# Groups 0 to 4 plain with all attention units among them, and two pairs of groups at the end, in a fused attention and token/channel mixer on one core

## The chip, the core and the metric

The kernel runs on one core of a Trainium2 chip. A core has TensorE (PE: matmuls, with weight loads shown apart as PEld), VectorE (DVE), ScalarE (ACT), GpSimd (POOL) and SyncE (SP), which here issues most DMAs. Engines run their instructions in order, each its own queue, and wait for each other through semaphores. SBUF is the on-chip memory, PSUM the eight accumulator banks that PE writes. The metric is the device time in microseconds of one execution; lower is better.

## The reference

Eight batches, eight heads, 576 rows, 64 columns a head. The attention is linear: softmax of q over the head's columns, softmax of k over the rows, then two small products. A mixer over tokens and a mixer over channels follow; all in fp32.

```python
q_s = softmax(q, axis=-1); k_s = softmax(k, axis=2)
kv = einsum('bhsd,bhse->bhde', k_s, v)
x = einsum('bhsd,bhde->bhse', q_s, kv)          # then (8, 576, 512)
h = np.maximum(x.transpose(0, 2, 1) @ w_tok1, 0.0) @ w_tok2      # 576 -> 256 -> 576
u = x + h.transpose(0, 2, 1)
h2 = np.maximum(u @ w_ch1, 0.0) @ w_ch2                          # 512 -> 1536 -> 512
out = u + h2
```

## The kernel before

The work has two halves. The first makes u in 32 *units*: a unit is one batch b and one slice j of 128 of the 512 channels (two heads). Its stages are the softmax of k and q (`softmax_k`, `softmax_q`: DVE, ACT, POOL), the transposed q (`stage_qT`, through DRAM for the later units), kv (`stage_kv`), y (`stage_y`), h1 (`stage_h1`) and two halves of u (`stage_u`). `begin` loads a unit two units ahead.

The second half is the channel mixer. The 8 x 576 rows of u are cut into nine *groups* of 512 rows, which do not fall together with the batches. For a group, ch1 gives 12 rows of 128 hidden channels (f = 0 to 11), ch2 adds them to the four output tiles of 128 channels. Each fp32 operand is kept as a high and a low part (`split`: ACT copies the high one, DVE subtracts it), and a product takes three matmuls (high x high, low x high, high x low). A plain ch1 of one f is 4 x 3 = 12 matmuls of 512 columns, a plain ch2 of one f as many. The main loop goes over `steps` (group, f): it issues ch1 of this step, then whatever `todo` holds for it (unit stages, put there by `put` with a step number), then ch2 of the step before. ch1's relu, high part on ACT and low part on DVE (lines 490 and 491), stands between the two.

Two by two blocks of a product can be had with seven products in place of eight (Strassen and Winograd's scheme), with sums of weight blocks and of data blocks. Weight blocks and their sums are made once and written to DRAM (`keep_blocks`, `keep_sums` for ch1, `keep_out`, `keep_out_sums` for ch2), and each product loads its weights, 256 KB, into a ring of buffers (`load_product`, `weights_used`). Before, this is used in two ways:

- Groups 0, 1 and 2 are plain in ch1 and ch2.
- Groups 3 to 6 (`G_S` = 3) use it in ch1 alone, and take the two blocks of data from the two halves of the same group: `pair_a` and `pair_b` do two f at a time by seven products of 6 matmuls on 256 columns, with five sums on DVE; ch2 is plain.
- Groups 7 and 8 use it in both, with the blocks from the two groups: `both_groups` does six pairs of f by seven products of 6 matmuls on 512 columns (part a), and then for each of seven products all six pairs (part b). Data sums are made ahead by `row_sum`, `data_sums`, `wide_sums` and `wide_split`; in part b `operand` makes each operand up to `AHEAD` products before its use.

The units run among the steps: batch 2 at two steps a unit, batches 3 to 7 at three steps a unit (line 1015), so up to the last of groups 2 to 6. The order within each engine comes from the framework's scheduler, which takes the program's order and its own estimate of durations; so an instruction can move past others, and the order is fixed before the kernel runs.

Of the kernel before, what the change touches and what calls it, by code (L numbers as in the profile page):

```python
# [20 lines left out]
def attn_mixer_kernel(ctx: ExitStack, tc: tile.TileContext, q, k, kt, v, wt, out, dims):  # L21
# [16 lines left out]
    G_S = 3  # L38
# [3 lines left out]
    KEEP = (5.5, 7.5, 37, 38.5, 40, 41.5)  # L42
    AHEAD = 12
# [11 lines left out]
    ps_o = ctx.enter_context(tc.tile_pool(name="ps_o", bufs=NJ, space=bass.MemoryType.PSUM))  # L55
    ps_h = ctx.enter_context(tc.tile_pool(name="ps_h", bufs=4, space=bass.MemoryType.PSUM))
# [54 lines left out]
    main_pools = ctx.enter_context(ExitStack())  # L111

    def c2_rows(f0, f1):
        late = main_pools.enter_context(tc.tile_pool(name=f"late{f0}", bufs=1))
# [9 lines left out]
    c2_rows(0, F_HEAD)  # L124
    part = const.tile([P, NJ, CW], F32, name="part")
# [42 lines left out]
    def load_unit(b, j):  # L168
        n = b * NJ + j
        u = {"b": b, "j": j, "n": n, "early": n < NE}  # L170
# [104 lines left out]
    whole = {}  # L275

    def load_pair(f):
# [6 lines left out]
        split(*(w[:, i : i + 2].rearrange("p f m -> p (f m)") for w in (wh, wl)), load_wide(AT_C2 + f), nc.vector)  # L284

    def load_ch(f):
# [6 lines left out]
        split(*c2_row(f), load_weights(AT_C2 + f), nc.vector)  # L293
# [149 lines left out]
    uT = [slots[i] for i in (0, 1, 2, 1, 0, 2, 1, 0, 2)]  # L443
    assert len(uT) == NG
# [3 lines left out]
    def stage_u(u, half):  # L448
# [16 lines left out]
        for g, a0, a1 in ((b, n0, min(n1, edge)), (b + 1, max(n0, edge), n1)):  # L465
            if a0 < a1:
                at = b * S + a0 - g * CW
                uh, ul = (x[:, j, at : at + a1 - a0] for x in uT[g])
# [57 lines left out]

    def keep_out(p):

        scratch_v[p] = dpool.tile([P, 7, 2, 2 * P], F32, name=f"v{p}")
# [5 lines left out]
    def keep_out_sums(p):  # L535

        hi = stg.tile([P, CW, 2], U32, name="stg").rearrange("p n w -> p (n w)").bitcast(F32R)
        lo = stg.tile([P, CW, 2], U32, name="stg").rearrange("p n w -> p (n w)").bitcast(F32R)
        a = f32(hi).rearrange("p (f m) -> p f m", f=2)
        (wh, wl), i = c2[2 * p]  # L540
        nc.gpsimd.tensor_tensor(a, f32(wh[:, i : i + 2]), f32(wl[:, i : i + 2]), op=ALU.add)
        s = f32(lo).rearrange("p (k m) -> p k m", k=4)
        (a11, a21), (a12, a22) = ([a[:, f, x * 2 * P : (x + 1) * 2 * P] for x in range(2)] for f in range(2))
# [5 lines left out]
        for x, w in enumerate((hi, lo)):  # L549
            nc.sync.dma_start(scratch_v[p][:, P5 : P3 + 1, x, :], f32(w).rearrange("p (k m) -> p k m", k=4))  # L550


    ring, T, tf, odd, h_slots = [], [], [], [], []

    def stage_pair_pools(f0):
        if f0 == F_MORE:
            c1_pools[F_LAST].close()
        c1_pools[f0].close()
        if f0 == 0:
            pool = ctx.enter_context(tc.tile_pool(name="pairs_a", bufs=1, side="right", reuse_waits="tile"))  # L560
# [12 lines left out]
    FIRST = (P1, P5, P2, P3, P6, P7, P4)
    GA, GB = NG - 2, NG - 1
    turn_of = [FIRST] + [TURN] * (NP - 1)
    loads = [(scratch_w, p, e) for g in range(G_S, GA) for p in range(NP) for e in TURN]
    n_main = len(loads)
    loads += [(scratch_w, p, e) for p in range(NP) for e in turn_of[p]]
    loads += [(scratch_v, p, e) for e in TURN for p in range(NP)]
    slot_of = [i % 8 if i < n_main else (i - n_main) % 6 for i in range(len(loads))]  # L580
    after, to_load, last_in = {}, [], {}
    for i, x in enumerate(slot_of):
        (after.setdefault(last_in[x], []) if x in last_in else to_load).append(i)
        last_in[x] = i

    def load_at_place(i):
        where, p, e = loads[i]
        nc.sync.dma_start(f32(ring[slot_of[i]].rearrange("p n m -> p (n m)")), where[p][:, e].rearrange("p x m -> p (x m)"))

    def load_product():  # L590
        load_at_place(to_load.pop(0))

    at_product, at_h = [0], [0]

    def next_weights():
        w = ring[slot_of[at_product[0]]]
        at_product[0] += 1
        return w

    def weights_used():  # L600
        for i in after.get(at_product[0] - 1, ()):
            load_at_place(i)

    rows = {}

    def rows_of(g):
        if g not in rows:
            if g % 2:
                rows[g] = [part[:, n : n + 2, :] for n in (0, 2)]
            else:  # L610
                rows[g] = [
                    stg.tile([P, CW, 2], U32, name="stg").rearrange("p n w -> p (n w)").bitcast(F32).rearrange("p (n w) -> p n w", n=2)
                    for _ in range(2)
                ]
        return rows[g]

    def row_sum(g, n, eng):
        uh, ul = (x[:, n, :] for x in uT[g])
        eng.tensor_tensor(rows_of(g)[n // 2][:, n % 2, :], f32(uh), f32(ul), op=ALU.add)

    A, Bq = slice(0, HW), slice(HW, CW)

    def data_sums(g, which):
        lo_rows, hi_rows = rows_of(g)
        b11, b12, b21, b22 = lo_rows[:, :, A], lo_rows[:, :, Bq], hi_rows[:, :, A], hi_rows[:, :, Bq]
        f0, f1 = (halves(x) for x in tf)
        sub = ALU.subtract
        for i in which:
            o, a, b = ((f0, b12, b11), (f1, b22, f0), (f0, b22, b12), (f0, b21, f1))[i]
            nc.vector.tensor_tensor(o, a, b, op=sub)  # L630
            split(T[0][:, i], T[1][:, i], tf[i == 1], nc.vector)

    def product(g, e, t, cols):
        w = next_weights()
        uh, ul = uT[g]
# [527 lines left out]
```

## Time and profile before

| | |
|---|---|
| three runs | 794.04, 794.77, 797.56 us (median 794.77) |
| the profiled execution | 796.62 us, of which the span from the first to the last instruction is 794.8 us |
| granted TensorE clock | 0.998 of full |
| bytes moved by DMA | 174.83 MB, 220 GB/s over the span |

In the profile, a group of instructions is shown by line, engine, operation and its tiles (out<-in); a tile's buffer numbers are left out. Matmuls overlap in the pipeline, so the duration of one is longer than the pace of a row of them; the pace is read from start to start, or from a chain of a known count. Idle time of an engine is given with what released it.

The page's slices of the span (40, each 19.9 us), in tenths of busy time:

```profile
PE   3899999999999999999999999999999999999998
...
DVE  7979998978788874878688657888987557667971
```

### The profile page before, as it was taken

What the parts mean: (1) busy time and instruction counts of PE and PEld (TensorE: products, weight loads), DVE (VectorE), ACT (ScalarE), POOL (GpSimd) and SP (SyncE); (2) the same over time, 40 slices, a digit from 0 to 9 for tenths busy, and PEclk for the clock granted to TensorE, in tenths of its full rate; (3) what the DMA queues carried; (4) which work ended last, traced back from release to release, by engine and by line L of the source; (5) the groups of instructions that cost most, each with busy time, mean ns of one, the idle gap of its engine ahead of it and who ended that gap; (6) DMA issues with size and microseconds to landing.
All of it is one profiled execution on the core that took longest, in us unless ns stands there. A gap on an engine that the chain in (4) does not pass through costs nothing.

```text
span 794.8 us, 13455 instructions
## 1 busy us (share of the span) xinstructions
PE 769.0 (97%) x4824; PEld 670.9 (84%) x4824; DVE 618.1 (78%) x1101; ACT 341.9 (43%) x744; POOL 180.7 (23%) x130
## 2 busy tenths in 40 slices
PE   3899999999999999999999999999999999999998
PEld 2688888877888888899999999989999998888886
DVE  7979998978788874878688657888987557667971
ACT  4666433444454443434353334434444324346610
POOL 0000000011111352122211111232422320536640
PEclk9999999999999999999999999999999999999999
DMA  9655644158879785587879777999978543667776
GB/s 304 187 174 166 224 150 171 44 171 278 273 243 336 232 286 177 144 282 210 238 213 287 226 219 216 288 339 314 316 233 270 161 134 115 195 189 198 192 207 196
DMA packets 151459, 174.83 MB, mean 220 GB/s; under 512 B 51297, under 2 KB 98017, under 8 KB 151393
## 3 DMA queue, kind: packets, MB, share of 16 engines
q1 hardware_dynamic: 145056, 161.65, 67.2%
q10 hardware_dynamic: 6336, 12.32, 4.1%
q8 instruction: 38, 0.62, 0.3%
q14 instruction: 29, 0.23, 0.1%
HBM read 131.47 MB, written 42.47 MB: 219 GB/s over the span
## 4 chain that ended last, share of the span: by engine, by line
PE 70%; DVE 11%; issue 7%; DMA 7%; ACT 2%; POOL 1%; SPq 1%; DVEq 0%; POOLq 0%; ACTq 0%
PE ps_o L694 20%; PE ps_h L645 14%; PE ps_h L768 7%; PE ps_o L768 7%; PE ps_h L464 6%; PE ps_h L422 4%; PE ps_h L487 4%; PE ps_h L357 2%; DMA q_t<-in_q 2%; DMA stg<-whole 1%; PE ps_h L430 1%; PE ps_o L464 1%; PE ps_o L882 1%; DMA w<-stg 1%; DVE q_t L340 1%
## 5 line engine op out<-in xcount | busy, mean ns | idle before, releaser
L694 PE MATMUL ps_o<-h,c2h 128*128 128x512 f32 x544 | 184.2, 398 | 2.9 <-ACT h L490 1.9
L694 PEld LDWEIGHTS ps_o<-h,c2h 128*128 128x128 f32 x544 | 101.4, 188 | 23.8 <-ACT h L490 3.0
L694 PE MATMUL ps_o<-h,c2l 128*128 128x512 f32 x272 | 106.0, 393 | 0.0
L318 POOL TENSOR_TENSOR k_t<-k_t,dg 128x640 f32<-128x640 f32 x24 | 41.6, 1735 | 217.6 <-ACT dg L317 182.1
L135 POOL TENSOR_TENSOR ql<-q_t,qh 128x640 fp32r<-128x640 f32 x24 | 38.4, 1599 | 182.3 <-PE ps_o L694 104.2
L645 PE MATMUL ps_h<-th,ring 128*128 128x256 f32 x384 | 72.3, 283 | 0.0
L645 PEld LDWEIGHTS ps_h<-th,ring 128*128 128x128 f32 x384 | 60.1, 191 | 0.0
L694 PEld LDWEIGHTS ps_o<-h,c2l 128*128 128x128 f32 x272 | 51.3, 188 | 8.6
L487 PE MATMUL ps_h<-uh,c1l 128*128 128x512 f32 x144 | 56.2, 390 | 0.0
L487 PE MATMUL ps_h<-ul,c1h 128*128 128x512 f32 x144 | 56.2, 390 | 0.0
L487 PE MATMUL ps_h<-uh,c1h 128*128 128x512 f32 x144 | 56.1, 392 | 0.0
L645 PE MATMUL ps_h<-uh,ring 128*128 128x256 f32 x288 | 54.4, 282 | 0.6 <-DVE c L672 0.6
L645 PE MATMUL ps_h<-tl,ring 128*128 128x256 f32 x192 | 54.3, 283 | 0.0
L645 PEld LDWEIGHTS ps_h<-uh,ring 128*128 128x128 f32 x288 | 46.5, 190 | 2.8 <-DVE c L672 0.8
L471 ACT CAST uh<-ps_h 128x320 fp32r<-128x320 f32 (+4 forms) x76 | 24.4, 334 | 52.1 <-PE ps_h L464 32.1
L336 ACT ACTIVATE q_t<-q_t 128x640 f32<-128x640 f32 x32 | 23.6, 738 | 46.1 <-DVE q_t L327 43.1
L326 DVE TENSOR_REDUCE st<-q_t 128x10 f32<-128x640 f32 x32 | 26.1, 815 | 22.2 <-DMA q_t<-in_q 22.2
L490 ACT ACTIVATE h<-ps_h 128x512 fp32r<-128x512 f32 x36 | 21.5, 598 | 49.5 <-PE ps_h L487 42.0
L645 PE MATMUL ps_h<-ul,ring 128*128 128x256 f32 x144 | 40.6, 282 | 0.0
L645 PEld LDWEIGHTS ps_h<-tl,ring 128*128 128x128 f32 x192 | 36.8, 192 | 0.0
L472 DVE TENSOR_TENSOR ul<-ps_h,uh 128x320 fp32r<-128x320 f32 (+4 forms) x76 | 27.4, 370 | 9.0 <-ACT uh L471 8.8
L135 DVE TENSOR_TENSOR qtl<-q_t,qth 128x512 fp32r<-128x512 f32 (+1 forms) x48 | 25.6, 566 | 8.1 <-ACT qth L134 7.3
(319 smaller groups left out, 2070.2 us busy)
## 6 DMA issues: line engine op xcount, KB each, us to landing
ring<-w SPq DMA_DIRECT2D x210, 256.0 KB, 3.7
ring<-v SPq DMA_DIRECT2D x42, 256.0 KB, 3.0
kt_t<-in_kt SPq DMA_DIRECT2D x32, 320.0 KB, 3.7
q_t<-in_q SPq DMA_DIRECT2D x32, 320.0 KB, 3.7
v_t<-in_v SPq DMA_DIRECT2D x32, 320.0 KB, 4.5
stg_w<-in_w SPq DMA_DIRECT2D x18, 512.0 KB, 6.0
k_t<-in_k SPq DMA_DIRECT2D x24, 320.0 KB, 4.9
q<-cv_s SPq DMA_DIRECT2D x24, 320.0 KB, 3.2
```

The costliest lines, as they stand in the source:

```text
L135: lo_eng.tensor_tensor(lo, src, f32(hi), op=ALU.subtract)
L318: nc.gpsimd.tensor_tensor(kx, kx, dg.unsqueeze(1).broadcast_to([P, C1, P]), op=ALU.subtract)
L326: nc.vector.tensor_reduce(st[:, 0, :], qt, axis=AX.X, op=ALU.max)
L336: nc.scalar.activation(qc, qc, AF.Exp)
L422: nc.tensor.matmul(y[:, 0:TOK], a, w, start=(i == 0), stop=(i == len(mm) - 1))
L464: nc.tensor.matmul(t[:, 0:N], a, w, start=(i == 0), stop=(i == len(mm) - 1))
L471: nc.scalar.copy(uh, src).ins,
L472: nc.vector.tensor_tensor(ul, src, f32(uh), op=ALU.subtract).ins,
L487: nc.tensor.matmul(t, a[:, n, :], w, start=(i == 0), stop=(i == 3 * NJ - 1))
L645: nc.tensor.matmul(t[:, cols], a, b[:, n], start=(i == 0), stop=(i == 5))
L694: m = nc.tensor.matmul(o, a[:, cs], w, start=(first and i == 0), stop=(last and i == 2))
L768: nc.tensor.matmul(o, a, b, start=first and i == 0 and (n == 0 or not one), stop=last and i == 2 and (n == 1 or not one))
```

## The change

The uses of the seven products are changed. `G_S` becomes 5: groups 0 to 4 are plain in ch1 and ch2, and the last four groups are two pairs, (5, 6) and (7, 8), both by `both_groups`, which is called for round 0 and round 1. `pair_a`, `pair_b` and their pools are gone. What moves with it:

- Units: batches 3 to 6 run at two steps a unit, all within the steps of groups 2 to 4 (36 steps); batch 7's four units run among the items of round 0, a unit every 12 items (`SPACE`). An item is one product of 6 matmuls; a round has 84.
- u of groups 5 to 8 is not split in `stage_u` but copied by ACT (`stay`) and written to DRAM (`u_kept`); `make_first`, `make_second` and `make_third` load it, make the data sums and split them. For round 0 that is in the last steps of group 4; for round 1 in the last part of round 0. The residual is loaded again (`residuals`).
- In a round, the products that share an accumulator add up in PSUM (P1, P6, P7, P4 in one bank, P5 and P3 in another, P2 in a third), with copies of the partial sums in between; before, each product had a bank of its own and DVE summed them. Six banks serve the products, two the units (`bank_pools`).
- Operands of part b take the places of u and of a part of c2; the differences for P6 and P4 are made by POOL when they are needed; `AHEAD` is 9 for 12. Parts a and b interleave by a fixed list (`items`).
- c2's pieces are also written to DRAM when they are loaded (`whole_out`), and `keep_out_sums` reads them back; POOL's sum for it is gone. The steps at which blocks and sums are kept change (`BLOCKS1`, `SUMS1`, `BLOCKS2`, `SUMS_AT`).

```diff
-    G_S = 3
+    G_S = 5
+    NR = (NG - G_S) // 2
-    KEEP = (5.5, 7.5, 37, 38.5, 40, 41.5)
-    AHEAD = 12
+    AHEAD = 9
+    SUMS_AT = (6.5, 11.5, 16.5, 21.5, 26.5, 29.5)
+    BLOCKS1, SUMS1, BLOCKS2 = (18, 20, 22, 24, 26, 28), (20.5, 24.5, 28.5, 32.5, 37.5, 42.5), (6, 11, 16, 21, 26, 29)
+    RES_AT = 31
+    SPACE = ((7, 8, 1, 12), (8, 8, 0, 0))
...
     def load_ch(f):
...
-        split(*c2_row(f), load_weights(AT_C2 + f), nc.vector)
+        t = load_weights(AT_C2 + f)
+        split(*c2_row(f), t, nc.vector)
+        if f % 2 == 0:
+            whole_out[f // 2] = dpool.tile([P, 2 * CW], F32, name=f"out{f}")
+        nc.scalar.dma_start(whole_out[f // 2][:, f % 2 * CW : (f % 2 + 1) * CW], t.bitcast(F32))
...
+                if g >= len(uT):
+                    if g not in u["kept"]:
+                        u["kept"][g] = [at, at, stay()]
+                    k0, k1, x = u["kept"][g]
+                    nc.scalar.copy(x[:, k1 - k0 : k1 - k0 + a1 - a0], t[:, a0 - n0 : a1 - n0])
...
+    TURN = (P1, P5, P6, P2, P7, P3, P4)
+    items = [("a", 0, e) for e in TURN[:5]]
+    for p in range(1, NP):
+        items += [("a", p, P1), ("a", p, P5), ("a", p - 1, P4), ("a", p - 1, P3), ("a", p, P6), ("a", p, P2), ("a", p, P7)]
+    tail = [("b", c, e) for e in TURN for c in range(NP)]
+    items += tail[:2] + [("a", NP - 1, P4), ("a", NP - 1, P3)] + tail[2:]
...
+    def make_first(r):
+
+        g = G_S + 2 * r
+        ready[r] = []
+        for k in range(2):
+            b11, b12, b21, b22 = (h_of[2 + i][:, 1] if k and r else row_place() if i or r else sum_place() for i in range(4))
+            for t, (i, n) in ((b11, (0, k)), (b12, (1, k)), (b22, (1, 2 + k)), (b21, (0, 2 + k))):
+                nc.sync.dma_start(t, u_kept[g + i][n])
+            t0 = sum_place()
+            t1 = sum_place() if r else b11
+            split(*of_first[k], b11, nc.vector)
+            vec(t0, b12, b11, op=sub)
+            split(*of_T[0][k], t0, nc.vector)
+            vec(t1, b22, t0, op=sub)
+            split(*of_T[1][k], t1, nc.vector)
+            split(*of_second[k], b21, nc.vector)
+            vec(b12, b22, b12, op=sub)
+            vec(b21, b21, t1, op=sub)
+            ready[r].append((b12, b21, b22))
...
+        def operand():
...
+            if e in (P6, P4):
+                t = sum_place()
+                pl(t, h[:, 3], h[:, 0], op=sub)
+                if e == P4:
+                    pl(t, h[:, 2], t, op=sub)
...
+            if not end and kind == "b" and done_b[0] == N_MOST:
+                make_first(r + 1)
+            if not end and kind == "b" and done_b[0] == N_MOST + 8:
+                make_second(r + 1)
...
-    steps += [(g, f) for g in range(2, GA) for f in range(NF)]
+    steps += [(g, f) for g in range(2, G_S) for f in range(NF)]
...
+        elif b < 7:
+            at = [n0 + -1 + 2.0 * (n - 3 * NJ) + x for x in (0, 0.5, 1, 1.5, 2)]
         else:
-            at = [n0 - 1 + (b - 3) * NF + 3 * j + x for x in (0, 0.5, 1, 1.5, 2)]
+            break
...
-    both_groups()
+    hidden_pools()
+    bank_pools()
+    make_second(0, (3,))
+    for r in range(NR):
+        both_groups(r, laters[r])
```

Three places show how the order on an engine moves. The first is PE at the start of group 3. Before, it runs the products of `pair_a` (`uh`, `ul`: the parts of u; `th`, `tl`: the parts of the data sums; `ring`: the loaded weights):

```order
L645 MATMUL ps_h<-uh_125,ring_3103 128x256 x2
L645 MATMUL ps_h<-ul_126,ring_3103 128x256
L645 MATMUL ps_h<-uh_125,ring_3103 128x256 x2
L645 MATMUL ps_h<-ul_126,ring_3103 128x256
L645 MATMUL ps_h<-th,ring_3104 128x256 x2
L645 MATMUL ps_h<-tl,ring_3104 128x256
```

At the same place in the changed kernel, group 3's first ch1 follows y of a unit (L437) and runs on 512 columns with the weights in SBUF (`c1h`, `c1l`):

```order
L437 MATMUL ps_h<-w1tl,qh 128x256
L517 MATMUL ps_h<-uh_125,c1h_115 128x512
L517 MATMUL ps_h<-uh_125,c1l_116 128x512
L517 MATMUL ps_h<-ul_126,c1h_115 128x512
L517 MATMUL ps_h<-uh_125,c1h_115 128x512
L517 MATMUL ps_h<-uh_125,c1l_116 128x512
```

The matmuls of 256 columns with loaded weights have become matmuls of 512 columns that load nothing from DRAM.

The second place is SP at the start of round 0 in the changed kernel. `u_129` to `u_132` are the rows kept in DRAM of groups 5 to 8, L812 is a residual, L637 a ring load, L195, L186 and L412 belong to units:

```order
L812 DMA part<-u_130 128x512
L812 DMA stg<-u_129 128x512
L812 DMA rows_5266<-u_130 128x512
L812 DMA rows_5265<-u_130 128x512
L195 DMA v_t<-in_v 128x10x64
L186 DMA k_t<-in_k 128x640
L412 DMA q_5920<-cv_s 128x4x160
L812 DMA part<-u_129 128x512
L812 DMA stg<-u_129 128x512
L637 DMA ring_5257<-w_1973 128x512
L812 DMA part<-u_129 128x512
L637 DMA ring_5258<-w_2145 128x512
```

The scheduler has moved the residual loads, which the program issues at item 31, to the start of the round, ahead of the first ring loads that follow the eight made before the round; `part` and `stg` are also the buffers from which group 4's output is written.

The third place is DVE in the last part of round 0, where the operands for round 1 are made (`c2l`, `ul`: low parts of operands; L823: output sums; L675, L678: data sums of `make_first`; `hb`: the hidden rows or rows of u in their place):

```order
L143 TENSOR_TENSOR c2l_121<-hb_5450,c2h_120 128x512
L143 TENSOR_TENSOR ul_126<-stg,uh_125 128x512
L823 TENSOR_TENSOR part<-b_5461,part 128x512
L823 TENSOR_TENSOR part<-b_5460,part 128x512
L143 TENSOR_TENSOR ul_126<-hb_5449,uh_125 128x512
L143 TENSOR_TENSOR ul_128<-sum_5270,uh_127 128x512
L143 TENSOR_TENSOR ul_128<-sum_5272,uh_127 128x512
L143 TENSOR_TENSOR ul_128<-sum_5269,uh_127 128x512
L143 TENSOR_TENSOR ul_126<-part,uh_125 128x512
L823 TENSOR_TENSOR part<-b_5462,part 128x512
L675 TENSOR_TENSOR sum_5271<-part,sum_5270 128x512
L678 TENSOR_TENSOR stg<-part,stg 128x512
```

From the second of these rows to the last split for round 1 stand 28 rows, six of them output sums (L823); in the kernel before no second pair follows, and the rows have no counterpart.

More of the change, by code (lines that the diff above doesn't have):

```diff
@@ L600, in weights_used @@
[L600 to L631, printed above, removed]
@@ new lines, in attn_mixer_kernel, with pair_pools @@
+    ring, spare_rows, sums, h_of = [], [], [], []
+    def pair_pools():
+        c1_pools[0].close()
+        pool = ctx.enter_context(tc.tile_pool(name="pairs_a", bufs=1, side="right", reuse_waits="tile"))
+        ring.extend(pool.tile([P, 4, P], F32R, name=f"ring{i}") for i in range(8))
+        spare_rows.extend(part[:, n, :] for n in range(NJ))
+        spare_rows.extend(pool.tile([P, CW], F32, name=f"rows{i}") for i in range(2))
+        stays[:] = (pool.tile([P, CW], F32, name=f"stay{i}") for i in range(2))
+        sums.extend(pool.tile([P, CW], F32, name=f"sum{i}") for i in range(4))
@@ L756, in attn_mixer_kernel @@
-    b21_of = {}
-    def wide_split(i, k):
-        src = (first_diff[k:], wide_sum[k:], beside[k:], [b21_of.get(k)])[i][0]
-        split(*wide_T(i, k), src, nc.vector)
-    def six(w, pieces_h, pieces_l, outs, first, last):
-        for n in range(2):
-            o = outs[n % len(outs)]
-            one = len(outs) == 1
-            for i, (a, b) in enumerate(((w[:, n], pieces_h[n]), (w[:, 2 + n], pieces_h[n]), (w[:, n], pieces_l[n]))):
-                nc.tensor.matmul(o, a, b, start=first and i == 0 and (n == 0 or not one), stop=last and i == 2 and (n == 1 or not one))
@@ new lines, in bank_pools, with relu, six @@
+    def bank_pools():
+        banks.close()
+        pool = ctx.enter_context(tc.tile_pool(name="bk", bufs=1, space=bass.MemoryType.PSUM))
+        t = {i: pool.tile([P, CW], F32, name=f"b{i}") for i in (2, 3, 5, 4, 0, 1)}
+        places.extend(t[i] for i in range(6))
+        pu = ctx.enter_context(tc.tile_pool(name="pu", bufs=2, space=bass.MemoryType.PSUM))
+        unit_banks[0] = ((pu, "pu"),)
+    def relu(c):
+        nc.scalar.activation(c, c, AF.Relu)
+    def six(w, pieces_h, pieces_l, outs, first, last, which=(0, 1)):
+        one = len(outs) == 1
+        for n in which:
+            for i, (a, b) in enumerate(((w[:, n], pieces_h[n]), (w[:, 2 + n], pieces_h[n]), (w[:, n], pieces_l[n]))):
+                nc.tensor.matmul(
+                    outs[0 if one else n], a, b,
+                    start=first and i == 0 and (n == 0 or not one),
+                    stop=last and i == 2 and (n == 1 or not one),
+                    skip_group_check=True,
+                )
@@ L794, in operand, with both_groups @@
+    at_product = [0]
+    def both_groups(r, later):
+        ga = G_S + 2 * r
+        end = r == NR - 1
+        sets = [places[0:2], places[2:4]]
+        made, done_b, hidden = [0], [0], [0]
+        order = [(c, e) for _, c, e in tail]
         def operand():
             i = made[0]
[L796 removed]
+            if i == len(order):
                 return
[L798 removed]
+            c, e = order[i]
             made[0] += 1
[L800 removed]
@@ L908, in attn_mixer_kernel @@
+        if not end:
+            make_third(r + 1)
+        assert not later, later
     units = {}
```

520 lines of the change are left out of this document (219 added, 301 removed).

## The prediction

> **What bounds the kernel now.** I read the page's busy rows first, then the stretches of the span, then what TensorE (PE) waited for.
>
> ```profile
> span 794.8 us, 13455 instructions
> PE 769.0 (97%) x4824; PEld 670.9 (84%) x4824; DVE 618.1 (78%) x1101; ACT 341.9 (43%) x744; POOL 180.7 (23%) x130
> ```
>
> PE is busy for all but 25.8 us. The next view cuts the span by stage; its columns are the stretch, its length, and the busy time (and instructions) of PE, PE's weight loads, VectorE (DVE), ScalarE (ACT) and GpSimd (POOL), then the granted clock, the DMA share and GB/s.
>
> ```profile
> 0.00:78.00 78.00, 60.18 (x445) 50.74 (x446) 66.44 (x151) 48.66 (x113) 1.94 (x17) 0.98 0.68 212
> 78.00:155.00 77.00, 77.00 (x353) 64.22 (x353) 72.88 (x109) 32.98 (x53) 3.62 (x2) 1.00 0.42 148
> 155.00:240.00 85.00, 81.99 (x501) 68.49 (x500) 70.19 (x130) 38.93 (x88) 13.47 (x8) 1.00 0.76 233
> 240.00:331.70 91.70, 91.49 (x539) 77.51 (x539) 68.90 (x122) 39.25 (x86) 29.34 (x18) 1.00 0.75 236
> 331.70:669.00 337.30, 336.10 (x2451) 308.93 (x2451) 258.26 (x481) 135.77 (x328) 80.00 (x49) 1.00 0.79 242
> 669.00:735.00 66.00, 66.00 (x296) 54.79 (x296) 44.81 (x64) 30.74 (x52) 31.17 (x24) 1.00 0.65 182
> 735.00:794.80 59.80, 56.25 (x249) 46.24 (x247) 36.59 (x49) 15.55 (x28) 21.15 (x13) 1.00 0.69 199
> ```
>
> The idle time lies in the first 78 us (17.8), in 155 to 240 (3.0) and at the end (3.5). The clock is full. In 331.7 to 669 (groups 3 to 6) PE loses 1.2 us, in 669 to 735 nothing. So the kernel is bound by the number and pace of its matmuls, and the change is worth what it does to those, less every gap that it opens. All gaps behind 155 us but the tail are these, in order of time (idle time and releaser in brackets):
>
> ```profile
> 165.02 0.50 PE L694 MATMUL ps_o<-h,c2h 128*128 128x512 f32 x1 [0.96 <-ACT h L490]
> ...
> 173.69 0.50 PE L694 MATMUL ps_o<-h,c2h 128*128 128x512 f32 x1 [0.76 <-ACT h L490]
> ...
> 193.87 1.20 PE L694 MATMUL ps_o<-h,c2h 128*128 128x512 f32 x4 [1.00 <-DVE h L491]
> ```
> ```profile
> 529.28 0.50 PE L645 MATMUL ps_h<-uh,ring 128*128 128x256 f32 x2 [0.62 <-DVE c L672]
> ...
> 534.41 0.50 PE L464 MATMUL ps_h<-w2h,hl 128*128 128x256 f32 x2 [0.59 <-DVE hl L438]
> ```
>
> (0.5 us of tiny ones apart.) In a plain group PE waits for the relu of the hidden rows, when ACT or DVE come to it late.
>
> **The change, part by part.**
>
> 1. *The width of the products.* Before, groups 3 to 6 do ch1 by seven products on 256 columns: 4 groups x 6 pairs of rows x 7 x 6 = 1008 matmuls.
>
> ```profile
> L645 PE MATMUL ps_h<-th,ring 128*128 128x256 f32 x384 | 72.3, 283 | 0.0
> L645 PE MATMUL ps_h<-uh,ring 128*128 128x256 f32 x288 | 54.4, 282 | 0.6 <-DVE c L672 0.6
> L645 PE MATMUL ps_h<-tl,ring 128*128 128x256 f32 x192 | 54.3, 283 | 0.0
> L645 PE MATMUL ps_h<-ul,ring 128*128 128x256 f32 x144 | 40.6, 282 | 0.0
> ```
>
> 384+288+192+144 = 1008. Their durations overlap, so I take the pace from the chain that ended last, where 24 in a row stand with their sum:
>
> ```profile
> 331.91 2.87 PE ps_h L645 x24
> ...
> 698.77 5.44 PE ps_h L768 x24
> ```
>
> A matmul of 256 columns takes 119.6 ns, one of 512 takes 226.7. In columns nothing is saved: before, 3 plain groups x 288 + 4 x (126 + 144) + 504 = 2448 matmuls of full width; after, 5 x 288 + 2 x 504 = 2448. The seventh product is won on one more ch2 pair and given back by two plain ch1. What is left is width: 1008 x 0.1196 = 120.6 us become 504 x 0.2267 = 114.3: **-6.3 us**. (The Trainium skill speaks against this: "TensorE: Matmul & The Clock Gate", section "Back-to-back issue gap", gives an isolated matmul N/2.4 ns and about 2.5 ns more. By it 504 pairs save 504 x 2.5 ns = 1.3 us, and the sum below would be 5.0 us later. The trace's paces differ from it, 119.6 and 226.7 ns against its 109.2 and 215.8.)
>
> 2. *ch2 between narrow products.* Starts of ch2 between such products:
>
> ```profile
> 642.36 0.40 PE L694 MATMUL ps_o<-h3h,c2l 128*128 128x512 f32 x1
> ...
> 644.66 0.39 PE L694 MATMUL ps_o<-h3l,c2h 128*128 128x512 f32 x1
> ```
>
> Ten steps in 2.30 us are 230 ns each. The 288 matmuls of ch2 of groups 5 and 6 become products at 226.7: **-1.0** (bounds 0 and -2.0, if groups 3 and 4 gain it too).
>
> 3. *Gaps that go.* The two at 529 and 534 lie in work that is gone: **-1.2**. What could be late in their place is part 5.
>
> 4. *Loading.* load_pair and load_ch now also write each c2 piece to DRAM, so cv buffers are held longer.
>
> ```profile
> whole<-cv_s ACTq DMA_DIRECT2D x4, 256.0 KB, 3.7
> ```
>
> That is c1's copy now, and this is what DVE waited for it, 0.5 us in all:
>
> ```profile
> L395 DVE STREAM_TRANSPOSE cv_s<-q_t 128x640 f32<-128x640 f32 x24 | 20.1, 837 | 0.7 <-DMA whole<-cv_s 0.5
> ```
>
> DVE is busy 72.88 of 77 us in 78 to 155, so what is late there stays late. Four more such copies: the far end is 4 x (3.7 - 0.7) = 12 us, if DVE had nothing beside the split (0.7) to do meanwhile; but it works on the other buffer. I take the nearest row: **+0.5** (0 to 12; below nothing only by another order, of which I see no sign).
>
> 5. *Plain groups with all units among them.* Groups 2 to 4 are 36 steps, 864 x 0.2267 = 195.9 us. A unit's own PE time follows from groups 3 to 6: 337.3 - 120.6 - 576 x 0.230 = 84 us for 16 units, 5.3 each. So 16 units in plain groups make a stretch of 281 us with one unit in two steps, where it was three. Before ran two-step spacing in batch 2 alone:
>
> ```profile
> 158.00:198.00 40.00, 37.21 (x217) 30.31 (x216) 33.60 (x60) 16.92 (x39) 6.28 (x4) 1.00 0.72 224
> 198.00:238.00 40.00, 39.78 (x248) 34.29 (x247) 32.11 (x63) 19.86 (x45) 7.19 (x4) 1.00 0.84 258
> ```
>
> It lost 2.79 and 0.22 us of 40. Two of the first window's gaps (165, 173.7) lie where load_ch still runs; I take the second: 281 / 40 x 0.22 = **+1.5**, with ends 0 and 281 / 40 x 2.79 = 19.6. The far end is a rival below.
>
> 6. *Into round 0.* SP issues eight residual rows, some into buffers that wait for the output of group 4, ahead of the second set of ring loads.
>
> ```profile
> ring<-w SPq DMA_DIRECT2D x210, 256.0 KB, 3.7
> ...
> out<-part ACTq DMA_DIRECT2D x14, 256.0 KB, 4.5
> ```
>
> The cover is eight loaded products, 8 x 6 x 0.2267 = 10.9 us, and two units' PE time. Four sums of 0.69 (row in 8), 4.5 to land and 3.7 to load are 11.0 after the last ch2: **0**, up to +3.
>
> 7. *Units among products.* Products now add up in one PSUM bank, so a product waits for ACT's copy of the one before it; the order leaves two to three products, 2.7 to 4.1 us, between. The longest operation of a unit on DVE and a copy from PSUM on ACT:
>
> ```profile
> L340 DVE TENSOR_TENSOR q_t<-q_t,st 128x640 f32<-128x640 f32 x32 | 30.1, 942 | 0.4
> ```
> ```profile
> L836 ACT COPY hb<-ps_o 128x512 f32<-128x512 f32 x4 | 2.3, 582 | 0.0
> ```
>
> 0.58 and 0.94 fit into 2.7; three long operations ahead of a copy do not (3.4). Nothing to two gaps like that at 193.87 (1.00) in each of four units are 0 to +8; I take one gap in all, as two-step spacing gave one in 178 to 240: **+1.0**.
>
> 8. *The turn to round 1.* While P7, P3 and P4 of round 0 end, DVE must make the operands of round 1.
>
> ```profile
> L135 DVE TENSOR_TENSOR ul<-hb,uh 128x512 fp32r<-128x512 f32 x10 | 9.4, 967 | 1.8 <-ACT uh L134 1.8
> ...
> L904 DVE TENSOR_TENSOR stg<-ps_o,stg 128x512 f32<-128x512 f32 x2 | 1.4, 692 | 6.8 <-PE ps_o L768 6.8
> ...
> L135 DVE TENSOR_TENSOR x2l<-hb,x2h 128x512 fp32r<-128x512 f32 x1 | 0.7, 681 | 0.0
> ```
> ```profile
> L135 DVE TENSOR_TENSOR tl<-tb,th 128x512 fp32r<-128x512 f32 x4 | 4.7, 1207 | 0.0
> ```
>
> From the split of the first new row (its place is read by product 23 of the 42) DVE has 28 rows: six output sums and 22 operations between SBUF tiles. At 0.69 they take 19.3 us, at 0.967 25.4, at 1.207 30.7. PE has 19 products, 25.8 us. So 0 to 30.7 - 25.8 = +4.9; by the middle row it just fits: **+1.0**.
>
> Round 1 is like the old last pair (66.00 of 66.00 busy) with fewer sums on DVE, and the tail is the same. DVE loses the five sums of pair_a and pair_b in 24 places; that only widens cover.
>
> Sum: -6.3 - 1.0 - 1.2 + 0.5 + 1.5 + 0 + 1.0 + 1.0 = **-4.5 us**. The profiled execution took 796.62 us (span 794.8, 1.8 around it) and would take 792.1. The median of the runs is 794.77, 1.85 below the profiled one; so I predict **790.3 us**. 0.5% is 4.0 us, about what a measurement of this kernel can tell from no change.
>
> **Rivals.**
>
> - *All cover holds* (parts 4 to 8 at nothing): -8.5, **786.3**. For it: 669 to 735 without a gap, 0.2 us lost in 240 to 331.7. Against: no row has units among wide products.
> - *The turn binds* (part 8 at 1.207): 790.3 + 3.9 = **794.2**. For it: DVE operations with both inputs in SBUF are slow in the rows above while POOL subtracts (967 and 1207 against 681), and POOL makes the 12 differences for P4 in the turn. It decides from 25.8 / 28 = 0.92 us for a mean operation. (The Trainium skill's "GPSIMD Engine Reference", section "8. Key points", says that POOL shares its SBUF interfaces with DVE, with contention for DVE instructions with two SBUF inputs; the 692 of a sum with one input in PSUM, and the 967 of a split, agree.)
> - *One unit in two steps starves the plain groups*: DVE, busy 33.60 of 40 there, comes late to the relu (L491), and each 40 us lose 2.79: 790.3 - 1.5 + 19.6 = **808.4**, slower. It is slower than before from (794.8 - 788.8) / 7.0 = 0.86 us lost in 40, and by over 0.5% from 1.4. Against: 198 to 238, at the same spacing, lost 0.22.
> - *The load is uncovered* (part 4 at its end): 790.3 + 11.5 = **801.8**. Against: the 0.5 us of its row.
> - *Width saves nothing*: a matmul's fixed part is 2.5 ns, and wide products run at 2 x 119.6 - 2.5 = 236.7 ns: -1.3 for -6.3, **795.3**. That is the page's formula as a mechanism; the 226.7 of 24 wide products in a row speaks against it.
>
> **How the numbers follow.** Forecast 0.54 (its own range 787.5 to 792.5; 0.43 faster by over 0.5%, 0.11 within); all cover holds 0.09 (faster); turn 0.20 (within); starved plain groups 0.12 (0.10 slower, 0.02 within, where only part of it comes); load 0.02 (slower); width 0.03 (within). Faster 0.52, within 0.36, slower 0.12. The range takes in the covered case (with 1.0 more of part 2) and the ends of parts 6 to 8 one at a time (790.3 + 7.0 for part 7), and leaves out the 0.12 of the two slower cases: 785 to 798.
>
> **What would show it.** Products of 512 columns at 226.7 ns and none of 256 in ch1; PE losing under 2 us in the plain groups behind 200 us, its gaps released by the relu pair of ch1 (L520 and L521 by the new lines); one gap of about 1 us, or none, at the turn; DVE at about 0.9 us an operation there; no wait of PE for a ring load at the start of round 0. A gap in most steps of groups 2 to 4 would prove me wrong.

## The result, and the profile after

The changed kernel takes 805.1 us (median of 6 runs, 804.1 to 809.4) against 795.3 for the kernel before (6 runs, 794.0 to 797.6): a ratio of **1.0144, with a 95% interval of 1.0117 to 1.0170**. It is slower by 10 to 11 us (the medians are 9.8 apart, the ratio makes it 11.4), where 790.3 (785 to 798) was forecast. The profiled execution took 805.2 us.

The busy row of the page, after:

```profile
span 803.4 us, 12255 instructions
...
PE 766.9 (95%) x4320; PEld 644.3 (80%) x4320; DVE 572.6 (71%) x958; ACT 376.7 (47%) x794; POOL 177.0 (22%) x129
```

PE has the 504 matmuls fewer that were forecast and is busy 2.1 us less; DVE is busy 45 us less. But PE's idle time has grown from 25.8 to 36.5 us. The stretches say where (stretch, length, busy time of PE, its weight loads, DVE, ACT, POOL, then granted clock, DMA share, GB/s):

```profile
147.00:200.00 53.00, 46.77 (x245) 37.36 (x244) 43.08 (x77) 21.55 (x47) 6.47 (x4) 0.94 0.60 187
200.00:250.00 50.00, 49.95 (x315) 42.64 (x314) 37.98 (x71) 21.48 (x49) 8.18 (x5) 1.00 0.83 256
250.00:350.00 100.00, 96.56 (x612) 82.31 (x612) 67.77 (x123) 45.70 (x107) 18.81 (x12) 1.00 0.64 197
350.00:450.00 100.00, 97.05 (x607) 83.83 (x606) 69.08 (x124) 44.81 (x105) 18.98 (x12) 1.00 0.72 216
450.00:543.00 93.00, 92.98 (x541) 79.16 (x540) 66.49 (x113) 41.67 (x94) 18.34 (x12) 1.00 0.69 216
543.00:643.00 100.00, 99.64 (x569) 84.37 (x568) 59.26 (x89) 59.32 (x126) 41.98 (x28) 1.00 0.73 217
643.00:683.00 40.00, 38.28 (x168) 31.09 (x167) 30.88 (x41) 15.34 (x26) 12.17 (x8) 1.00 0.87 284
683.00:740.00 57.00, 55.75 (x245) 45.56 (x244) 21.63 (x30) 28.04 (x48) 16.14 (x12) 1.00 0.75 223
```

Three places lose time. From 147 to 200 (the end of loading) PE is idle 6.2 us, and the clock is at 0.94 besides; from 250 to 450 (plain groups) 6.4; from 643 to 740 (the turn) 3.0. At the start of round 0 and among its products (543 to 643), 0.4. What PE waited for, in the view of its waits (us in all, times, longest):

```profile
PE ps_h L331 <- DVE h L521: 3.5, 4, 1.4
PE ps_h L485 <- ACT qth L142: 3.1, 1, 3.1
...
PE b L743 <- DMA ring<-w: 1.0, 2, 0.6
```

The products themselves run as forecast. From the chain that ended last:

```profile
584.35 5.46 PE b L743 x24
```

Twenty-four in 5.46 us are 227.5 ns each. With every matmul at the median step of its kind (from start to start), PE's work adds up to 748.0 us before and 740.8 after, 7.2 less. Its busy time falls by less because slower matmuls, those at half the clock among them, count as busy too.

The largest single loss is at 180 us. PE's timeline there, and at three later gaps (start, length, engine, line, operation; in brackets the idle time before and its releaser):

```profile
180.16 0.63 PE L485 MATMUL ps_h<-qth,kvh 128*128 128x320 f32 x1 [3.14 <-ACT qth L142]
180.59 0.63 PE L517 MATMUL ps_h<-uh,c1h 128*128 128x512 f32 x1
181.02 0.63 PE L517 MATMUL ps_h<-uh,c1l 128*128 128x512 f32 x1
...
382.96 0.49 PE L331 MATMUL ps_h<-dg,ones 128*128 128x128 f32 x2 [0.94 <-DVE h L521]
...
400.00 0.49 PE L331 MATMUL ps_h<-dg,ones 128*128 128x128 f32 x2 [0.59 <-DVE h L521]
...
417.67 0.49 PE L331 MATMUL ps_h<-dg,ones 128*128 128x128 f32 x2 [1.43 <-DVE h L521]
```

After a pause of 3.1 us the matmuls start every 0.43 us and not every 0.227: the twelve of the next ch1 run at half the clock, which costs 12 x 0.2 = 2.4 us on top of the pause. What PE waited for is the q of a unit. Its transposed form goes through a buffer `cv_s`, out to DRAM and back. DVE there and at 382 us, and ACT:

```profile
160.28 0.43 DVE L242 TENSOR_SCALAR cv_s<-stg 128x512 uint32<-128x512 uint32 x1 [1.60 <-DMA whole<-cv_s]
...
172.04 0.83 DVE L410 STREAM_TRANSPOSE cv_s<-q_t 128x640 f32<-128x640 f32 x1
...
174.35 0.84 DVE L410 STREAM_TRANSPOSE cv_s<-q_t 128x640 f32<-128x640 f32 x1 [0.86 <-DMA out<-cv_s]
...
381.54 0.43 DVE L579 TENSOR_TENSOR stg<-stg 128x256 f32<-128x256 f32 x1 [4.62 <-DMA stg<-out]
381.88 0.42 DVE L581 TENSOR_TENSOR stg<-stg 128x256 f32<-128x256 f32 x1
382.22 0.69 DVE L521 SCALAR_TENSOR_TENSOR h<-ps_h,h 128x512 fp32r<-128x512 f32 x1
```
```profile
179.49 0.62 ACT L142 CAST qth<-q_t 128x512 fp32r<-128x512 f32 x1 [5.49 <-DMA q_t<-q]
```

The second transpose waited 0.86 us for the new copy of a c2 piece (`out<-cv_s`) to leave that buffer, and before that the conversion of a weight piece had waited 1.60 us for c1's copy (`whole<-cv_s`); before the change DVE waited 0.5 us for such copies in all. The rows of DVE at 382 are one of the gaps in the plain groups, which stand where operand sums of c1 and c2 (keep_sums, keep_out_sums) are formed. DVE stood for 4.6 us at the head of its queue, waiting for a c2 copy to come back from DRAM; the eviction of a ch1 bank (L521) came behind it, and PE's gap at 382.96 ends with it.

So the theory that went into the experiments was this. **A**: the copies cost at loading (they hold `cv_s`) and again when they are read back. **B**, its rival: one unit in two steps is too dense by itself, and the gaps fall where they fall. **D**: at the turn DVE is slow because GpSimd works beside it; its rival, that DVE has too much to do there.

### The profile page after: what moved, and what is told of

The parts are those of the page before. It is cut to its first block, busy times and chain, and to the rows that moved or that the text cites. A ratio compares the mean times of both kernels' runs of the same rounds, so it can differ in the third digit from the quotient of the medians.

```text
span 803.4 us, 12255 instructions
## 1 busy us (share of the span) xinstructions
PE 766.9 (95%) x4320; PEld 644.3 (80%) x4320; DVE 572.6 (71%) x958; ACT 376.7 (47%) x794; POOL 177.0 (22%) x129
## 4 chain that ended last, share of the span: by engine, by line
PE 65%; DVE 13%; DMA 9%; issue 6%; ACT 3%; POOL 2%; SPq 1%; DVEq 0%; POOLq 0%; ACTq 0%
PE b L743 25%; PE ps_h L517 13%; PE ps_o L699 12%; PE ps_h L485 4%; PE ps_h L437 3%; DMA q_t<-in_q 3%; DMA stg<-out 1%; PE pu L485 1%; DMA q_t<-q 1%; PE ps_h L372 1%; SPq L414 1%; PE ps_o L485 1%; DMA ring<-w 1%; POOL ql L143 1%; PE pu L437 1%
## 5 line engine op out<-in xcount | busy, mean ns | idle before, releaser
L743 PE MATMUL b<-uh,ring 128*128 128x512 f32 x480 | 148.7, 391 | 3.0 <-DVE rows L823 1.1
L743 PEld LDWEIGHTS b<-uh,ring 128*128 128x128 f32 x480 | 89.2, 188 | 22.5 <-DVE rows L823 1.5
L517 PE MATMUL ps_h<-uh,c1l 128*128 128x512 f32 x240 | 95.1, 396 | 0.1
L743 PE MATMUL b<-ul,ring 128*128 128x512 f32 x240 | 93.0, 390 | 0.0
L521 DVE SCALAR_TENSOR_TENSOR h<-ps_h,h 128x512 fp32r<-128x512 f32 x60 | 40.9, 682 | 31.8 <-ACT h L520 31.6
L517 PEld LDWEIGHTS ps_h<-ul,c1h 128*128 128x128 f32 x240 | 45.6, 190 | 9.8
L517 PEld LDWEIGHTS ps_h<-uh,c1h 128*128 128x128 f32 x240 | 45.7, 190 | 9.0 <-DVE ul L502 0.5
L517 PEld LDWEIGHTS ps_h<-uh,c1l 128*128 128x128 f32 x240 | 45.7, 190 | 8.9 <-DVE c1l L143 0.6
L743 PEld LDWEIGHTS b<-ul,ring 128*128 128x128 f32 x240 | 45.1, 188 | 9.5
L143 DVE TENSOR_TENSOR ul<-hb,uh 128x512 fp32r<-128x512 f32 x40 | 42.3, 1091 | 6.4 <-ACT uh L142 5.4
```

The costliest lines, as they stand in the source:

```text
L143: lo_eng.tensor_tensor(lo, src, f32(hi), op=ALU.subtract)
L517: nc.tensor.matmul(t, a[:, n, :], w, start=(i == 0), stop=(i == 3 * NJ - 1))
L521: nc.vector.scalar_tensor_tensor(hl, t, 0.0, f32(hh), op0=ALU.max, op1=ALU.subtract).ins,
L743: nc.tensor.matmul(outs[0 if one else n], a, b, start=first and i == 0 and (n == 0 or not one), stop=last and i == 2 and (n == 1 or not on ...
```

## The experiments

Ratios are to the kernel before, each measured on the same chip in the same session; 0.001 of it is 0.8 us.

**No copies at all.** The c2 copies are not written at loading, and the sums take c2 from its two halves in SBUF, as the kernel before did:

```diff
-        whole_out[f // 2] = dpool.tile([P, 2 * CW], F32, name=f"out{f}")
-        nc.scalar.dma_start(whole_out[f // 2], t.bitcast(F32))
...
-        nc.sync.dma_start(f32(hi), whole_out[p])
+        nc.gpsimd.tensor_tensor(a, f32(wh[:, i : i + 2]), f32(wl[:, i : i + 2]), op=ALU.add)
```

> The copies of the c2 pieces (whole_out) are neither written while c2 loads nor read back; the sums are formed from the hi and lo halves in SBUF by GpSimd, as the kernel before did. Theory A (the copies cost twice: at loading they hold the two cv_s buffers, and later each read back stands at the head of VectorE's queue with the eviction of a ch1 bank behind it): the 3.1 us gap at 180 us and the half clock behind it go (about -5.9 us), and the waits on stg<-out with them (about -3 us): about 796 us. Theory B (the spacing of the units, one in two steps, leaves too little slack on every engine): nothing changes beyond 1 us, 804 to 806 us. Theory C (GpSimd's additions cost as much through SBUF as the copies did): 801 to 805 us.

798.1 us (10 runs), ratio 1.0049 (1.0027 to 1.0071): 0.0095 less than the changed kernel, 7.6 us.

```profile
147.00:200.00 53.00, 50.93 (x302) 42.22 (x301) 47.26 (x87) 23.91 (x51) 6.35 (x4) 1.00 0.64 202
...
250.00:350.00 100.00, 98.74 (x631) 85.29 (x630) 67.93 (x123) 44.27 (x103) 21.26 (x13) 1.00 0.61 184
350.00:450.00 100.00, 97.70 (x614) 83.85 (x613) 71.03 (x120) 45.80 (x108) 23.98 (x14) 0.98 0.67 206
450.00:543.00 93.00, 91.25 (x528) 76.55 (x527) 69.42 (x112) 38.00 (x88) 21.77 (x13) 1.00 0.65 203
```

```profile
168.29 0.84 DVE L405 STREAM_TRANSPOSE cv_s<-q_t 128x640 f32<-128x640 f32 x1 [0.70 <-DMA whole<-cv_s]
```

From 147 to 200 the idle time falls from 6.2 to 2.1 us and the clock is full. The first transpose of that q comes 102.51 us after the first c1 piece was converted (at 65.78 us); in the changed kernel it came 107.05 us after it (at 64.99), 4.5 us later. But from 250 to 543 PE still loses 5.3 us. The copies are most of the loss; the plain groups have another.

**Copies written, not read**: the first two lines of that diff undone, the last two kept.

> The copies are written at loading as in the changed kernel, but nothing reads them; the sums are formed from the halves in SBUF by GpSimd. Theory A: the gap at 180 us and the half clock stay, only the waits on stg<-out go, so about 802 us, some 6 us above the run without any copies. Theory A with the load as its only part: 805 us. If the reads back are the whole cost: 796 us. Theory B: 804 to 806 us.

807.6 us, 1.0183 (1.0149 to 1.0217); in the same session the run without copies took 798.1. The two runs differ only in writing the copies, and that costs 9.5 us, no less than the run without copies gained; not reading them shows no gain over the changed kernel: A's second half falls.

**Copies read a step earlier**, in the changed kernel:

```diff
+            put(n0 + x - 1.0, lambda p=p: read_out(p))
             put(n0 + x, lambda p=p: keep_out_sums(p))
```

> The copies are written and read, but each read back is issued one step (about 8 us) ahead of the additions that use it. Theory A: VectorE finds the piece there, the idle time of VectorE on stg<-out (up to 4.6 us a time) goes, and with it the PE gaps at 382 and 416 us: about 802 us, the same as with the copies unread. Theory B: 804 to 806 us. If GpSimd's additions are what helps or hurts, this run and the one with the copies unread differ by over 1 us.

805.1 us, 1.0147 (1.0118 to 1.0175), no change. The edit did little of what it was for: DVE's wait for the copies fell from 12.4 to 10.2 us only. By itself it decides nothing; with the run before it, it says that these waits are not where the time is.

**The copies in the kernel before**, with nothing that reads them:

```diff
+        whole_out[f // 2] = dpool.tile([P, 2 * CW], F32, name=f"out{f}")
+        nc.scalar.dma_start(whole_out[f // 2], t.bitcast(F32))
```

> The kernel before, with the one addition that each c2 piece is also copied to DRAM while it loads (nothing reads the copies). Theory A (the copies hold cv_s, q comes back late, PE stands still for 3 us and then runs at half clock): the same gap near 177 us here, 3 to 7 us longer than the kernel before, 797 to 801 us. If the copies cost only together with the other parts of the change: 794 to 795 us.

801.1 us, 1.0073 (1.0049 to 1.0096): 5.8 us.

```profile
147.00:200.00 53.00, 47.54 (x250) 38.25 (x249) 44.31 (x79) 22.23 (x47) 6.47 (x4) 0.94 0.62 194
...
250.00:350.00 100.00, 97.23 (x587) 82.97 (x587) 76.09 (x130) 39.99 (x90) 28.80 (x19) 1.00 0.74 229
```
```profile
PE ps_h L471 <- ACT qth L134: 3.5, 1, 3.5
```

The same wait for the same q, and the same clock of 0.94, in a kernel that has nothing else of the change. That the copies cost at loading is shown. It is not all that they cost: from 250 to 350 us PE loses 2.8 us here, and in the kernel before, without the copies, 0.2:

```profile
250.00:350.00 100.00, 99.79 (x628) 85.94 (x627) 74.43 (x131) 39.37 (x89) 30.55 (x19) 1.00 0.74 235
```

Why stays open.

**Copies from the large buffers only.** load_ch's four copies from `cv_s` go, load_pair's from `cv_w` stay.

```diff
         t = load_weights(AT_C2 + f)
         split(*c2_row(f), t, nc.vector)
-        if f % 2 == 0:
-            whole_out[f // 2] = dpool.tile([P, 2 * CW], F32, name=f"out{f}")
-        nc.scalar.dma_start(whole_out[f // 2][:, f % 2 * CW : (f % 2 + 1) * CW], t.bitcast(F32))
```

> The changed kernel with the copies of c2 only where load_pair writes them from the large buffers (rows 0 to 7, read back as before); the four copies of load_ch from cv_s go, and the sums of those two pairs of rows are formed from the halves. If the cost at loading is the hold on cv_s, which the units' transposed q needs too: no gap of 3 us near 177 us, clock 1.00 from 147 to 200 us, 798 to 800 us. If it is the additional DMA traffic as such, or the copies from the large buffers: the gap stays, 803 to 805 us.

803.5 us, 1.0101 (1.0059 to 1.0144): against the changed kernel no gain that the intervals show. The pause for the q did go, but another stands in its place:

```profile
168.26 0.80 PE L702 MATMUL ps_o<-h,c2h 128*128 128x512 f32 x1 [3.71 <-ACT h L517]
```

Now the relu of the hidden rows is late, behind the conversion of a weight piece in ACT's queue. That the remaining copies make this pause is not shown: in the run without sums (the next one), which writes no copies at all, PE waits 2.7 us for the same relu:

```profile
PE ps_o L675 <- ACT h L515: 2.9, 2, 2.7
```

Nor is it shown that the large pieces come in later because of the copies. Here the first c1 piece and a later one are converted (L249) at 66.69 and 115.89 us, 49.2 apart; without copies it is 47.2. But it is 47.1 in the changed kernel, which has the pause, and 49.1 in the run with the chains cut in pieces (below), which has no copies and no pause above 1.7 us while it loads. So the pause at 180 us of the changed kernel goes with the copies from `cv_s`. What the copies from the large buffers cost by themselves, and whether any of them cost by their traffic or by their place in the queues, was not separated.

**No sums.** Without the copies, and the twelve chains of operand sums replaced by plain writes from SBUF, so that the products take other weights (it times the kernel without this work):

```diff
-        nc.vector.tensor_tensor(s[:, 0], a21, a22, op=ALU.add)
-        nc.vector.tensor_tensor(s[:, 1], s[:, 0], a11, op=ALU.subtract)
...
-        split(hi, lo, f32(lo), nc.vector)
+                nc.sync.dma_start(scratch_w[p][:, P5:P7, x, :], f32(w0).rearrange("p (k n) m -> p k (n m)", k=2))
```

> Without the copies, and the operand sums of c1 and c2 (keep_sums, keep_out_sums) are not formed: in their place SyncE writes rows of c1 and c2 from SBUF, so the products take other weights and the output is not the reference's. VectorE, ScalarE and GpSimd lose this work in the plain groups, everything else stays. Against the run without copies alone (798 us). Theory S (the twelve chains of sums, VectorE to ScalarE to VectorE, put waits into both queues ahead of a unit's or ch1's work): the idle time of PE from 250 to 543 us falls from 5.3 to under 1.5 us, and the half clock at 398 us goes: 792 to 794 us. Theory B (one unit in two steps is too dense in itself): 4 us or more of it stay, 796 to 799 us.

791.1 us, 0.9945 (0.9923 to 0.9967): 0.0104 less than without copies alone, 8.3 us.

```profile
250.00:350.00 100.00, 100.00 (x638) 86.72 (x638) 62.30 (x114) 43.31 (x103) 19.23 (x12) 1.00 0.68 207
350.00:450.00 100.00, 100.00 (x638) 86.50 (x637) 61.71 (x107) 43.40 (x107) 19.26 (x12) 1.00 0.67 202
450.00:543.00 93.00, 92.53 (x540) 78.58 (x539) 57.36 (x96) 41.27 (x96) 18.22 (x12) 1.00 0.70 226
```

Sixteen units, one in two steps, and PE loses 0.5 us in 293. Theory B falls: the spacing by itself costs next to nothing. The loss goes with the chains. But they don't cost it by themselves either: the kernel before forms the same twelve, seven of them between 200 and 290 us, and lost 0.4 us from 200 to 350.

**The chains cut in pieces**, same work, without the copies. The pieces also stand at other steps, so that two chains are 2.5 steps apart or more:

```diff
-        put(SUMS1[p], lambda p=p: keep_sums(p))
+        for stage_no, d in enumerate((-0.5, 0, 1, 1.5)):
+            put(SUMS1[p] + d, lambda p=p, k=stage_no: keep_sums(p, k))
...
+        with behind(drained):
+            nc.scalar.copy(hi, f32(lo))
```

> Without the copies; the twelve chains of sums are the same work, each cut in four pieces over two steps (reading, additions, the cast on ScalarE, the low half on VectorE), each piece placed behind the eviction of the ch1 bank of its step, and spaced 2.5 steps apart. Against the run without copies alone (798 us). If the chains cost by waits at the head of a queue (theory S1): the idle time from 250 to 543 us falls from 5.3 to 1 to 2 us, the half clock at 398 us goes: 793 to 795 us. If they cost by the work itself, some 3 us of VectorE for each chain (theory S2): 796 to 799 us, 4 us or more of idle time stay, spread otherwise.

796.4 us, 1.0026 (1.0003 to 1.0049), 1.8 us better, between the two theories; the intervals overlap.

```profile
250.00:350.00 100.00, 98.04 (x625) 84.15 (x624) 76.92 (x131) 44.99 (x105) 24.81 (x14) 1.00 0.71 216
350.00:450.00 100.00, 98.09 (x625) 84.53 (x624) 72.63 (x126) 47.35 (x111) 24.12 (x14) 1.00 0.70 211
450.00:543.00 93.00, 92.28 (x535) 78.10 (x534) 67.46 (x112) 40.52 (x92) 23.47 (x14) 1.00 0.68 215
```

4.6 us of the 5.3 are still idle; the clock of 0.98 from 350 to 450 is full again, which is about what the run gained. So, as far as this edit tells, what waits at the head of a queue explains little; the rest goes with the chains' work itself, and through which engine was not found.

**GpSimd's differences on VectorE**, in the changed kernel:

```diff
-                pl(t, h[:, 3], h[:, 0], op=sub)
+                vec(t, h[:, 3], h[:, 0], op=sub)
                 if e == P4:
-                    pl(t, h[:, 2], t, op=sub)
+                    vec(t, h[:, 2], t, op=sub)
```

> The differences for the operands of P6 and P4 (18 operations in each of the two rounds) move from GpSimd to VectorE. Theory D (at the turn between the rounds GpSimd and VectorE share a path to SBUF: splits out of hb take 1.8 us beside GpSimd's work and 0.69 us alone): splits fall to 0.69 us, the gaps of 3 us at the turn fall to 1 to 2 us, 803 to 804 us. Theory E (VectorE has too much to do at the turn, whatever its pace): 18 x 0.6 us more for it in each round, about half of that between products, gaps at the turn of 5 us or more, 807 us or above.

803.7 us, 1.0137 (1.0103 to 1.0170): no difference that the intervals show. The split is faster, as theory D has it. Groups of instructions (busy us, mean ns; idle time before and its releasers), of the changed kernel first, then of this one:

```profile
L143 DVE TENSOR_TENSOR ul<-hb,uh 128x512 fp32r<-128x512 f32 x40 | 42.3, 1091 | 6.4 <-ACT uh L142 5.4 <-PE b L743 0.6 <-issue 0.2
L769 POOL TENSOR_TENSOR sum<-hb 128x512 f32<-128x512 f32 x24 | 37.4, 1563 | 40.9 <-DVE ul L143 28.4 <-DVE h L143 8.1 <-DVE sum L675 4.4
```
```profile
L143 DVE TENSOR_TENSOR ul<-hb,uh 128x512 fp32r<-128x512 f32 x40 | 29.5, 758 | 5.0 <-ACT uh L142 5.0
L769 DVE TENSOR_TENSOR sum<-hb 128x512 f32<-128x512 f32 x24 | 20.2, 850 | 5.0 <-POOL hb L776 4.8
```

But PE now waited 2.6 us at the turn for a ring load. A second cause stood behind the first.

**Residuals in the program's order.** Without the copies, the residual rows of round 1 are held behind the ring load that precedes them in the program:

```diff
+                    with behind(last_ask if r else []):
-                    nc.sync.dma_start(t, u_kept[ga + key[0]][2 * key[1] + m])
+                        nc.sync.dma_start(t, u_kept[ga + key[0]][2 * key[1] + m])
```

It is aimed at this, in the run without copies, on SyncE's queue and on PE:

```profile
668.98 0.42 SPq L634 DMA_DIRECT2D ring<-w  x1
671.74 0.32 SPq L809 DMA_DIRECT2D stg<-u  x1
672.11 1.38 SPq L634 DMA_DIRECT2D ring<-w  x3
```
```profile
673.68 0.78 PE L740 MATMUL b<-uh,ring 128*128 128x512 f32 x2 [2.40 <-DMA ring<-w]
674.26 0.63 PE L740 MATMUL b<-ul,ring 128*128 128x512 f32 x1
```

The residual (L809) waits for its buffer, three ring loads wait behind it, PE pauses for 2.4 us, and the clock halves again.

> Without the copies, and the residual rows of round 1 are asked for behind the ring load ahead of them in the program, and no more at the start of the round, where they wait for their buffers in SyncE's queue ahead of ring loads. Against the run without copies alone (798 us). Theory F (at the turn PE waits for weights that stand behind a residual in SyncE's queue): the wait of 2.4 us for ring<-w at 671 us and the half clock behind it go, 794 to 796 us. Theory D (VectorE, slowed by GpSimd, is late whatever the queue does): the wait turns into one for VectorE, 797 to 798.5 us.

799.8 us, 1.0057 (1.0035 to 1.0078): no gain. The wait of 2.4 us for a ring load is gone (PE is busy 39.10 of 40 us from 643 to 683, after 37.59). One of 1.3 us for another ring load stands at 729 us, and this is the largest wait for a product in its place, at 750 us:

```profile
PE b L740 <- DVE ul L143: 1.8, 1, 1.8
```

**Both at the turn**, without the copies.

> Without the copies, with the residual rows of round 1 behind their ring load and the differences for P6 and P4 on VectorE. Against the run without copies alone (798 us). If the two causes at the turn stand one behind the other (residuals in SyncE's queue first, splits slowed beside GpSimd second), only both together help: the gaps from 643 to 760 us fall from 3.2 us (and 1.4 us of half clock) to under 1.5 us, with splits out of hb at 0.69 us: 794 to 796 us. If VectorE's amount of work is the bound there, nothing is gained: 797 to 800 us.

793.7 us, 1.0001 (0.9976 to 1.0026): 3.8 us better than without copies alone. The residuals' order had gained nothing on the same base; the differences on VectorE had gained nothing in the changed kernel, and without copies they were not tried alone.

```profile
643.00:683.00 40.00, 40.00 (x178) 32.99 (x177) 28.67 (x46) 14.60 (x26) 0.00 (x0) 1.00 0.80 249
683.00:740.00 57.00, 57.00 (x253) 47.19 (x252) 30.17 (x43) 33.72 (x59) 16.34 (x11) 1.00 0.77 239
```

The turn has no gap left, although DVE took over 36 operations in the two rounds. Its amount of work was not the bound.

**All of it**: no copies, the chains in pieces, both edits at the turn.

> Both edits together, and no copies: if the causes add up (copies, chains, turn), 790 to 792 us, below the kernel before by 0.4 to 0.7%; if only the chains could be helped, 793 to 795 us; if neither, 797 to 800 us.

792.0 us, 0.9968 (0.9943 to 0.9994). Once more, in more rounds:

> The run with both edits and no copies once more, in more rounds, for the interval of its ratio to the kernel before: 0.994 to 0.999 if 0.9968 was right; an interval that holds 1 would mean that it only equals the kernel before.

792.1 us (12 runs), 0.9967 (0.9944 to 0.9990). This version beats both kernels: the changed one by 1.0144 - 0.9967 = 0.0177, 14 us, and the one before by a third of a per cent.

## Why the prediction was wrong

*What bounds the kernel* was right: what the change gained or lost is matmul time less the gaps that it opened.

*Parts 1 to 3 were right.* The median step of a product is 227 ns in the trace after and was 120 for the narrow ones: 1008 x 0.120 - 504 x 0.227 = 6.6 us, forecast 6.3. ch2's median step went from 229 to 227, and all median steps together give 7.2 us less, forecast 7.3. The two gaps at 529 and 534 left with their work. A tally from the other side comes out alike: what the copies (7.6), the chains (8.3) and the turn (3.8) cost comes to 19.7 us; taken from the 11.4 us by which the changed kernel is slower (0.0144), that leaves 8.3 faster, against the 8.5 of parts 1 to 3. It confirms little: it adds edits that were tried separately, each of the three differences is known only to within 2.5 to 2.8 us by the intervals of its two ratios, and it charges the chains to the change in full, though the kernel before forms them too and their cost there was not measured. That it comes so near is luck in part.

*Part 4, loading, is the first term that was mis-sized*: +0.5 forecast, 7.6 measured, inside its bounds of 0 to 12. The choice inside the bounds failed. The prediction stood right beside the reason: DVE was busy 72.88 of 77 us there, "so what is late there stays late". It then priced the copies by what DVE had waited for one such copy, 0.5 us, and "it works on the other buffer"; and it counted four more copies, where the change writes eight, four of 256 KB from `cv_s` and four of 512 KB from `cv_w`. In the changed kernel DVE's waits for copies out of `cv_s` were 1.60 and 0.86 us, the q was transposed 4.5 us later than without copies, PE stood still for 3.1 us, and the half clock, foreseen nowhere, added another 2.4. The rival of an uncovered load, with 801.8, was given a chance of 0.02 on the strength of that same row.

*Part 5, the plain groups, is the second*: +1.5 forecast; PE idles 6.5 us from 200 to 543 in the changed kernel's trace, at full clock, and the run without sums gained 8.3 over the run without copies, which ran at half the clock for a while there, too. Its mechanism was wrong as well as its size. It asked only how densely the units stand, and the spacing costs 0.5 us in 293. The twelve chains of sums appear in no term. The window of 198 to 238 that it took for a measure had three of them and lost 0.22; so a rate from there was not a rate for 293 us. The changed kernel itself lost 0.05 us from 200 to 250 with chains in it, and 6.4 from 250 to 450. What makes the later ones costly stays open. The rival that starves the plain groups (808.4) is as far from the measured time as that of the load (801.8), 3.3 us; PE did wait there for VectorE at the relu, as it says, but the reason that it gives, the spacing alone, is excluded by the run without sums.

*Part 6 was right*: at the start of round 0 PE waited for no ring load. *Part 7* forecast 1.0 and the trace has 0.4 from 543 to 643.

*Part 8, the turn, is the third*: +1.0 forecast; PE idles 3.0 us there in the changed kernel, and without the copies both edits together gained 3.8. The splits out of hb took 1091 ns on the mean of both rounds, above the border of 0.92 us that the rival named, yet DVE was busy only 30.88 of 40 us from 643 to 683: its amount of work was not the bound, and its lateness was one of two causes in a row. Part 6 counted the residuals in SyncE's queue for round 0, and the same residuals, of round 1, went uncounted at the turn, where they stand ahead of ring loads and wait for buffers.

The range failed for one reason above these: it took the ends of the unknown costs one at a time, and three of them came together.

## What to carry to other kernels

Where an engine is full over a stretch, price new work there by lateness carried to the next consumer and not by the wait that the profile shows now: here waits of 1.6 and 0.9 us stood before a pause of 3.1. Two causes of one stall can stand one behind the other; an edit that gains nothing may be half of one that gains. And a window of another stage gives a rate only for a stage that holds the same work: list what stands in it beyond the thing you price.

## What the hardware showed

The pause itself isn't all that PE loses. Behind the first 60 us of all these traces, no pause below 1.9 us (from the start of one matmul to that of the next) was followed by a slow stretch, three of eight from 1.9 to 2.3 us were, and all fourteen from 2.48 us up. Six to thirteen matmuls of 512 columns then start 427 ns apart (in one case they were of 256 columns, 213 ns apart): 2.4 us more for the twelve behind the pause at 180 us of the changed kernel. In the traces' records of the granted clock each such stretch at half the clock is 3.4 or 6.8 us long. The Trainium skill's "TensorE: Matmul & The Clock Gate", section "Part 1: The HAM clock gate", has the clock fall to half after an idle window of about 3.4 us that runs freely. The 427 ns agree with that rate; but a pause of 2.0 us, well under the window, was enough in the run without copies (a wait of 0.5 us followed before the clock fell), and one of 2.3 us in the run with the chains cut was not. What decides between them no run here shows.

A split of 128 x 512 with both inputs in SBUF (`ul<-hb,uh`, 40 of them in the changed kernel) lasts 677 to 696 ns in the 18 cases in which no GpSimd operation runs beside it, and 678 to 1797, on the mean 1424, in the 22 in which one does. With the differences on VectorE the mean of all 40 falls from 1091 to 758. VectorE needs 850 ns for one where GpSimd needed 1563. So VectorE took over 36 operations, 29.3 us of work, and was busy 574.6 us in all, against 572.6: what they cost, faster operations beside them paid.
